# Weights of a slot by plain transfers with a register's row number, and w2 split one slot ahead

## The chip, the cores and the metric

The kernel runs on one core of a Trainium2 chip. The metric is the device time of one execution in microseconds (us). The matrix unit (TensorE) is called PE here, VectorE DVE, ScalarE ACT, GpSimd POOL and SyncE SP.

## The reference

Four attention problems are computed whose softmax runs over channels, and the result goes through a mixture of experts. Tokens with a positive skip score are computed, each by the one expert that its gate prefers; the others pass unchanged.

```python
s = kn.transpose(0, 2, 1) @ qn / tau          # q, k normalised over tokens; 256 x 256 per problem
a = softmax(s); x = (v @ a).reshape(20224, 256)
do_compute = x @ w_skip > 0
e_idx, gate_w = argmax and largest softmax of x[do_compute] @ w_gate     # 8 experts
for e in range(8):
    h = np.maximum(xc[mask] @ w1[e], 0.0)     # w1[e] 256 x 1024
    y[mask] = gate_w[mask] * (h @ w2[e])      # w2[e] 1024 x 256
out[do_compute] = xc + y
```

## The kernel before, in words

The program has three parts.

**The planned part.** All work up to the first loop is written as tasks with costs, dependences and due times (class `Plan`), and a planner puts them in an order per engine before the program is built. It covers the attention (scores, softmax, products with v), the routing of each token to its expert, lists of tokens per expert in DRAM (`lst`), and 7 blocks of 512 tokens of the expert with the most tokens so far. At its end DVE computes tables of slots (`tables`): a slot is a run of tokens of one expert. `adi` holds where a slot's list begins, `wii` which rows of the weight arrays belong to it.

**The large loop** (line 432, `Large.loop`) runs over slots of 1024 tokens, in two halves of 512. It ran 6 times in the profile shown. `first` is x times w1 with ReLU, `second` is h times w2. Float32 operands are split into a high and a low part (`w1H`, `w1L`, `w2s`), by a cast on ACT and a subtraction on DVE, so that each product needs three matmuls.

**The small loop** (line 522, `Small.loop`) runs over the rest, in slots of up to 128 tokens, two slots (u = 0, 1) in an iteration. It ran 5 times, so 10 slots. A slot has two stages. In the first, 32 matmuls multiply by w1 (`v1r`, line 539, result `ph`), and ACT and DVE make `yH` and `yL` of the result. In the second, 16 matmuls multiply by the split w2 (`v2s`, lines 558 and 559, result `po`), with the next slot's rows transposed in their midst (line 494), and DVE adds the result to the rows (`yo`, lines 564 and 565).

**Where weights come from.** Each slot's w1 and w2 are 128 x 2048 float32, 1 MB each. They are fetched by `gather_w`, an indirect transfer that POOL issues: each partition gives its own row number (`wc`, `wd`), which DVE has copied out of `wii`. Where a slot has the same expert as the slot whose buffer it takes over, `wii` holds a number out of bounds, and nothing is moved. Token rows come by `gather_x` (`yg`, line 209) and go back by `scatter_x` (`out`, line 214), on POOL too. SP only loads the lists (`load_list`, line 227), whose place it reads into a register.

**What sets the order in the loops.** The bodies are written out in order, per engine, and cut into four stages by `tc.stage_boundary()`: in the small loop, each slot's two. No engine enters a stage before all engines have ended the stage before the last one, and a stage has ended on the engine that issues transfers only when they have landed. `behind(...)` says at which point of a stage an engine reports that the stage before has ended. Ahead of each loop, and behind it, all engines wait for each other.

In the small loop before, w2 of a slot is split (`split_w2`) in that slot's own first stage, into a single `v2s`. w2 of the next slot is gathered at the start of the first stage, w1 of the slot after next at the start of the second.

Of the kernel before, what the change touches and what calls it, by code (L numbers as in the profile page):

```python
# [20 lines left out]
P = 128  # L21
# [122 lines left out]
def attn_moe(ctx: ExitStack, tc: tile.TileContext, q, k, vt, tau, w_skip, w_gate, w1, w2, out):  # L144
# [83 lines left out]


# [9 lines left out]
    class Large:  # L239
# [126 lines left out]
        def ahead(self, cnt0):  # L366


            V.scalar_tensor_tensor(cnt0, cnt0, 512.0 * K0, iota8, ALU.is_ge, ALU.mult)
            e0 = tab.tile([P, 1], F32, name="e0")  # L370
            V.tensor_reduce(e0, cnt0, AX.X, ALU.min)
            start = tab.tile([P, E], F32, name="start")
            V.tensor_scalar(start, iota8, e0, 512.0 * K0, ALU.is_equal, ALU.mult)
            V.tensor_scalar(e0, e0, float(E), None, ALU.add)
            ad0 = tab.tile([P, 1], I32, name="ad0")
            V.tensor_scalar(ad0, e0, float(CAP), None, ALU.mult)
            V.tensor_scalar(e0, e0, float(E - 1), None, ALU.min)
            for w in (self.wc, self.wd):
                V.tensor_scalar(w, e0, float(P), pidx, ALU.mult, ALU.add)
            yield e0, start  # L380
            beside(load_list(ad0, 0, self.lN[:, : 4 * K0, :], 4 * K0, G), "first lists", "later lists")
            yield
# [33 lines left out]
        def next_loads(self, adi, wii):  # L416

            self.adi, self.wii = adi, wii
            for w in (self.wc, self.wd):
                V.tensor_copy(w, wii[:, 0:1])  # L420
            yield
            load_list(adi, 0, self.lN[:, :8, :], 8)
            yield
            self.take(0)
            gather_w(w1, self.w1r, self.wc)
            self.gather(0)
            yield
            gather_w(w2, self.w2r, self.wd)
            yield

        def loop(self):
            with tc.For_i(0, self.n, 1, iteration_sync="staggered", hint_engines=(mybir.EngineType.PE,)) as i, tc.manual_schedule():
                V.tensor_copy(self.wc, self.wii[:, ds(i + 1, 1)])
                V.tensor_copy(self.wd, self.wii[:, ds(i + 1, 1)])
# [3 lines left out]
                gather_w(w1, self.w1r, self.wc)  # L438
# [4 lines left out]
                gather_w(w2, self.w2r, self.wd)  # L443
# [21 lines left out]
    class Small:  # L465


        def __init__(self, adi, wii):
            self.adi, self.wii = adi, wii
# [4 lines left out]
            self.xg = tiles([P, C], F32, "yg")  # L474
            self.xr = tiles([P, C], F32, "yr")
            self.xT = tiles([P, 2, P], F32, "yT")
            self.w2s = wp.tile([P, NFB, 2, C], F32R, name="v2s")
            self.hH = wp.tile([P, NFB, P], F32R, name="yH")
            self.hL = wp.tile([P, NFB, P], F32R, name="yL")
            self.ob = tiles([P, C], F32, "yo")  # L480
            self.wc = tiles([P, 1], I32, "vc")
            self.wd = tiles([P, 1], I32, "vd")
# [4 lines left out]
            for u in range(U):  # L487
                V.memset(self.xg[u], 0.0)
                V.memset(self.ob[u], 0.0)
# [8 lines left out]
        def split_w2(self, u, c):  # L498
            f = slice(c * 2, c * 2 + 2)
            r = self.w2r[u][:, c * 512 : (c + 1) * 512].rearrange("p (f c) -> p f c", c=C)  # L500
            S.copy(self.w2s[:, f, 0, :], r)
            V.tensor_tensor(self.w2s[:, f, 1, :], r, self.w2s[:, f, 0, :], ALU.subtract)

        def load_rows(self):
# [5 lines left out]
            for u in range(U):  # L510
                V.tensor_copy(self.wc[u], self.wii[:, u : u + 1])
                V.tensor_copy(self.wd[u], self.wii[:, u : u + 1])
                gather_x(self.xg[u], first[u][:, 0, :])

        def load_weights(self):
            for u in range(U):
                gather_w(w1, self.w1r[u], self.wc[u])
                if u < U - 1:
                    gather_w(w2, self.w2r[u], self.wd[u])

        def loop(self):
            with tc.For_i(0, self.n, U, iteration_sync="staggered") as i, tc.manual_schedule():  # L522
                for u in range(U):
# [3 lines left out]
                    gather_w(w2, self.w2r[o], self.wd[o])  # L527
# [3 lines left out]
                    for g in range(2):  # L531
                        for c in (0, 1, 2) if g == 0 else (3,):
                            self.split_w2(u, c)
# [10 lines left out]
                        if g == 0:  # L544
                            behind(T, S, V, SP)
                            V.tensor_copy(self.wc[u], self.wii[:, ds(i + (u + U), 1)])
                            V.tensor_copy(self.wd[u], self.wii[:, ds(i + (u + U), 1)])
# [5 lines left out]
                    gather_w(w1, self.w1r[u], self.wc[u])  # L553
                    gather_x(self.xg[u], self.lN[u][:, 0, :])
                    behind(G)
                    po = psum["o", u % 2].tile([P, 512], F32, name="po")
                    for f in range(NFB):
                        T.matmul(po, self.hH[:, f, :], self.w2s[:, f, :, :], start=(f == 0), stop=False, skip_group_check=True)
                        T.matmul(po[:, :C], self.hL[:, f, :], self.w2s[:, f, 0, :], start=False, stop=(f == NFB - 1), skip_group_check=True)
# [267 lines left out]
    def tables(e0, start):  # L827
# [20 lines left out]
        for i, (ns, w, back) in enumerate(((S8, 1024, 1), (S1, 128, U))):  # L848
# [6 lines left out]
            if i == 1:  # L855
                V.tensor_scalar(ei[:, :U], ei[:, :U], float(E - 1), None, ALU.min)
# [21 lines left out]
            V.tensor_tensor(same[:, back:], ei[:, back:], ei[:, : ns - back], ALU.is_equal)  # L878
            if i == 0:
                V.tensor_tensor(same[:, 0:1], ei[:, 0:1], e0, ALU.is_equal)  # L880
            else:
                V.memset(same[:, :back], 0.0)
# [133 lines left out]
    large = Large()  # L1016
    rows, early, slots, nexts, smalls = large.ahead(cnt0), [], [], [], []
# [68 lines left out]
    def table_part():  # L1086
        if not slots:
            early.append(tables(*early[0]))
# [3 lines left out]
    for n, cost in enumerate((1.64, 0.7, 1.5, 1.2, 1.49, 1.9, 1.6)):  # L1092
# [6 lines left out]
    def next_part():  # L1099
        if not nexts:  # L1100
            nexts.append(large.next_loads(slots[0][0], slots[1][0]))
        next(nexts[0])

    n0 = add("V", 0.15, next_part, [t1, wg2])
    n1 = add("D", 0.1, next_part, [n0, listed, in_order["gat"]])
    n2 = add("G", 5.4, next_part, [n1, stored[NC - 1], *w1s, puts.get(K0 - 3)])
    n2d = add("D", 4.4, None, [n2])
    n3 = add("G", 1.05, next_part, [n2, done[K0 - 1]], due=now)
# [3 lines left out]
    split_weights(1, n2d, last_m1, due=now)  # L1112

    def open_small():
        in_b.close()
        smalls.append(Small(slots[0][1], slots[1][1]))
        smalls[0].load_rows()
# [6 lines left out]
    add("G", 3.2, lambda: smalls[0].load_weights(), [sm, n3], due=now + 5)  # L1124
# [8 lines left out]
    with tc.manual_schedule():  # L1133
# [9 lines left out]
        smalls[0].transposed(0)  # L1143
        smalls[0].n = slots[3]
        large.loop()
        keep_warm(6)
        smalls[0].loop()
# [37 lines left out]
```

## Time and profile before

| | us |
|---|---|
| median of 3 runs (lowest to highest) | 840.38 (836.22 to 846.71) |
| the profiled execution | 839.25 |
| its span, first to last instruction | 837.6 |
| PE busy in the span | 792.3 (95%) |
| large loop, six slots, first matmul at | 469.46 |
| small loop, ten slots, first matmul at | 752.65 |

The span is about 1.7 us shorter than the execution's own time. PE is busy nearly throughout, so a gain has to come from the places where it isn't: the ends of the three parts, and the small loop.

### The profile page before, as it was taken

Reading aid. Unit: us, or ns where it says so; the run is one execution under the profiler, and the core shown is the slowest. Engines: PE = TensorE matmul, PEld = TensorE weight load, DVE = VectorE, ACT = ScalarE, POOL = GpSimd, SP = SyncE. Lnnn points to the kernel's source line nnn. Section 1 sums busy time; section 2 is a strip of 40 time slices with the busy share of each in tenths; the row PEclk is TensorE's granted clock in tenths of the full one; section 3 lists DMA queues with packets and bytes.
Section 4 is the critical chain, followed back from the end, with each engine's and each line's share of the span. In section 5 each row is a group of like instructions: output and inputs, shape, how many; then the busy total and the mean of one; then the engine's idle time right before and its main releaser. Section 6 shows DMA issues by size and latency. Waiting matters only on the chain. (4 is left out here: it accounts for less than half of the span.)

```text
span 837.6 us, 13567 instructions
## 1 busy us (share of the span) xinstructions
PE 792.3 (95%) x4506; PEld 697.6 (83%) x4506; DVE 519.4 (62%) x1055; ACT 369.5 (44%) x583; POOL 431.4 (52%) x470
## 2 busy tenths in 40 slices
PE   7999999989989999999989799999999999988886
PEld 5888998979978888998878588888888888877876
DVE  4729759968958653654556646556555647456555
ACT  5449558749746323433313324233333324234544
POOL 3000377767577757556764653435343443426666
PEclk9999999999999999999999899999999999999999
DMA  8969869979554342420601511111111111107670
GB/s 321 394 247 365 330 211 316 402 272 361 179 176 127 104 126 65 138 89 27 173 8 46 191 54 47 44 44 51 50 44 44 51 50 34 41 26 256 251 274 4
DMA packets 58074, 126.37 MB, mean 151 GB/s; under 512 B 17556, under 2 KB 37804, under 8 KB 55472
## 3 DMA queue, kind: packets, MB, share of 16 engines
q1 hardware_dynamic: 17280, 62.99, 20.3%
q0 software_dynamic: 19520, 42.12, 15.2%
q10 hardware_dynamic: 21232, 20.72, 8.1%
q8 instruction: 23, 0.38, 0.2%
q14 instruction: 19, 0.16, 0.1%
HBM read 115.98 MB, written 32.59 MB: 177 GB/s over the span
## 5 line engine op out<-in xcount | busy, mean ns | idle before, releaser
L817 POOL DMA_INDIRECT lst<-pay,r_posi x160 | 181.4, 1134 | 171.4 <-DVE r_posi L814 123.8
L662 PE MATMUL s<-qt,kt 128*128 128x256 f32 x640 | 148.3, 384 | 6.9 <-DMA kt<-in_k 6.9
L214 POOL DMA_INDIRECT out<-xg,lc x78 | 79.3, 1016 | 130.2 <-DVE xg L345 113.1
L662 PEld LDWEIGHTS s<-qt,kt 128*128 128x128 f32 x640 | 119.7, 192 | 22.3 <-issue 7.2
L338 PE MATMUL po<-w2s,hH 128*128 128x512 f32 x384 | 136.5, 399 | 0.4 <-issue 0.4
L321 ACT ACTIVATE hH<-ph 128x512 fp32r<-128x512 f32 x96 | 57.5, 599 | 129.6 <-PE ph L318 129.6
L339 PE MATMUL po<-w2s,hL 128*128 128x256 f32 x384 | 107.2, 279 | 0.0
L735 PE MATMUL px<-aH,vH 128*128 128x266 f32 x320 | 99.8, 312 | 0.6 <-ACT xo L742 0.6
L322 DVE SCALAR_TENSOR_TENSOR hL<-ph,hH 128x512 fp32r<-128x512 f32 x96 | 66.4, 692 | 54.7 <-ACT hH L321 53.3
L209 POOL DMA_INDIRECT xg<-out,lc x80 | 84.0, 1049 | 30.4 <-issue 18.7
L737 PE MATMUL px<-aH,vL 128*128 128x266 f32 x320 | 93.1, 291 | 0.0
L736 PE MATMUL px<-aL,vH 128*128 128x266 f32 x320 | 92.7, 290 | 0.3 <-DVE aL L719 0.3
L338 PEld LDWEIGHTS po<-w2s,hH 128*128 128x128 f32 x384 | 72.1, 188 | 17.4 <-issue 0.8
L338 PE MATMUL px<-w2s,hH 128*128 128x512 f32 x224 | 79.9, 398 | 2.4 <-DVE hL L401 2.4
L316 PE MATMUL ph<-xH,w1H 128*128 128x512 f32 x192 | 76.0, 396 | 5.0 <-issue 5.0
L742 ACT COPY xo<-px 128x532 f32<-128x532 f32 x80 | 47.7, 602 | 66.1 <-PE px L737 66.0
L317 PE MATMUL ph<-xL,w1H 128*128 128x512 f32 x192 | 75.6, 394 | 0.0
L318 PE MATMUL ph<-xH,w1L 128*128 128x512 f32 x192 | 75.5, 393 | 0.0
L339 PEld LDWEIGHTS po<-w2s,hL 128*128 128x128 f32 x384 | 72.4, 188 | 0.4
L284 ACT CAST xH<-pt 128x512 fp32r<-128x512 f32 x40 | 22.3, 590 | 106.1 <-PE pt L282 106.0
L735 PEld LDWEIGHTS px<-aH,vH 128*128 128x128 f32 x320 | 62.0, 194 | 2.0 <-ACT xo L742 1.0
L339 PE MATMUL px<-w2s,hL 128*128 128x256 f32 x224 | 63.6, 284 | 0.0
(206 smaller groups left out, 1588.3 us busy)
## 6 DMA issues: line engine op xcount, KB each, us to landing
vf<-in_vt SPq DMA_DIRECT2D x32, 640.0 KB, 6.6
qt<-in_q SPq DMA_DIRECT2D x31, 640.0 KB, 7.5
kt<-in_k SPq DMA_DIRECT2D x31, 640.0 KB, 7.4
out<-xo ACTq DMA_DIRECT2D x12, 1280.0 KB, 7.0
lst<-pay,r_posi POOLq DMA_INDIRECT x160, 4.2
out<-xo ACTq DMA_DIRECT2D x4, 640.0 KB, 5.3
out<-xo ACTq DMA_DIRECT2D x4, 576.0 KB, 8.0
xg<-out,lc POOLq DMA_INDIRECT x80, 2.8
```

Source lines behind the costliest of these rows:

```text
L209: apart(G.indirect_dma_start(out=to, out_offset=None, in_=out[0:n, :], in_offset=IndirectOffsetOnAxis(ap=ls[:, 0:1], axis=0), bounds_check ...
L214: i = (G.indirect_dma_start(out=out, out_offset=IndirectOffsetOnAxis(ap=ls[:, 0:1], axis=0), in_=src, in_offset=None, bounds_check=NTOK - ...
L316: T.matmul(ph, self.w1H[:, fs], self.xH[:, kb, :], start=(kb == 0), stop=False)
L317: T.matmul(ph, self.w1H[:, fs], self.xL[:, kb, :], start=False, stop=False)
L318: T.matmul(ph, self.w1L[:, fs], self.xH[:, kb, :], start=False, stop=(kb == 1))
L338: T.matmul(po, self.hH[:, f, ts], self.w2s[:, f, :, :], start=(f == 0), stop=False, skip_group_check=True)
L339: T.matmul(po[:, :C], self.hL[:, f, ts], self.w2s[:, f, 0, :], start=False, stop=(f == NFB - 1), skip_group_check=True)
L662: T.matmul(sums[b][:, cb, :], kt[:, j % JH, cb * P : (cb + 1) * P], qt[:, j % JH, :], start=(ch == 0 and j == 0 and cb == 0), stop=(ch == ...
L735: T.matmul(px[:, i, :NA], vH[:, kb, js], aH[:, kb, :], start=(kb == 0), stop=False)
L736: T.matmul(px[:, i, :NA], vH[:, kb, js], aL[:, kb, :], start=False, stop=False)
L737: T.matmul(px[:, i, :NA], vL[:, kb, js], aH[:, kb, :], start=False, stop=(kb == 1))
L817: i = G.indirect_dma_start(out=lst, out_offset=IndirectOffsetOnAxis(ap=posi[:, t : t + 1], axis=0), in_=pay[:, t0 + t, :], in_offset=None, ...
```

## The change

Weights of slots are no longer gathered by POOL. `load_w` reads the slot's first row number into a register of SP and issues a plain transfer of 128 rows. `wii` now holds expert x 128, never out of bounds: each slot's weights are fetched, whatever the slot before had. Beyond the last slot the last expert's are fetched. The row numbers on DVE (`wc`, `wd`) and the comparison of experts are gone.

In the small loop `v2s` has two buffers. A slot's w2 is split in the second stage of the slot before, among the `po` matmuls, and slot 0's ahead of the loop. Transfers of w2 and of w1 both go to the slot after next. The transposes of the next slot stand one matmul pair earlier. The zeroing of row buffers moves to the program's start.

```diff
+    def load_w(ei, i, src, to):
+        a = nc.sync.value_load(ei[0:1, ds(i, 1)], min_val=0, max_val=(E - 1) * P)
+        nc.sync.dma_start(to, src[ds(a, P), :])
...
@@ Large.loop
-                V.tensor_copy(self.wc, self.wii[:, ds(i + 1, 1)])
-                V.tensor_copy(self.wd, self.wii[:, ds(i + 1, 1)])
                 self.put_last()
                 self.take(1)
                 self.gather(1)
-                gather_w(w1, self.w1r, self.wc)
+                load_w(self.ei, i + 1, w1, self.w1r)
                 behind(G, SP)
                 self.first(True)
                 tc.stage_boundary()
                 load_list(self.adi, i + 1, self.lN[:, :8, :], 8)
-                gather_w(w2, self.w2r, self.wd)
+                load_w(self.ei, i + 1, w2, self.w2r)
...
@@ Small.loop
+            for c in range(4):
+                self.split_w2(0, c)
             with tc.For_i(0, self.n, U, iteration_sync="staggered") as i, tc.manual_schedule():
...
-                    gather_w(w2, self.w2r[o], self.wd[o])
+                    load_w(self.ei, i + (u + U), w2, self.w2r[u])
                     G.tensor_copy(self.ls[o], self.lc[o])
                     scatter_x(self.ls[o][:, 0, :], self.ob[o])
                     behind(G)
                     for g in range(2):
-                        for c in (0, 1, 2) if g == 0 else (3,):
-                            self.split_w2(u, c)
...
                     tc.stage_boundary()
                     G.tensor_copy(self.lc[o], self.lN[o])
                     G.tensor_copy(self.lN[o], self.lP[o])
+                    load_w(self.ei, i + (u + U), w1, self.w1r[u])
                     load_list(self.adi, i + (u + 2 * U + 1), self.lP[o], 1)
                     behind(SP)
-                    gather_w(w1, self.w1r[u], self.wc[u])
                     gather_x(self.xg[u], self.lN[u][:, 0, :])
                     behind(G)
                     po = psum["o", u % 2].tile([P, 512], F32, name="po")
+                    for c in range(2):
+                        self.split_w2(o, c)
+                    behind(S, V)
                     for f in range(NFB):
...
+                        if f == 3:
+                            self.transposed(o)
+                            for c in range(2, 4):
+                                self.split_w2(o, c)
                         if f == 4:
-                            self.transposed(o)
-                            behind(T, S, V)
+                            behind(T)
...
@@ tables
-            wi = tab.tile([P, ns], F32, name=f"wi{i}")
-            V.tensor_scalar(wi, ei, float(P), pidx, ALU.mult, ALU.add)
-            same = tab.tile([P, ns], F32, name=f"same{i}")
...
-            V.scalar_tensor_tensor(wi, same, float(BIG), wi, ALU.mult, ALU.add)
             wii = tab.tile([P, ns], I32, name=f"wii{i}")
-            V.tensor_copy(wii, wi)
+            V.tensor_scalar(wii, ei, float(E - 1), float(P), ALU.min, ALU.mult)
...
@@ the planned part's end
+    nw = add("D", 2.9, lambda: load_w(slots[1][0], 0, w1, large.w1r), [t1, *w1s])
+    add("D", 2.9, lambda: load_w(slots[1][0], 0, w2, large.w2r), [nw, *w2s])
...
-    add("G", 3.2, lambda: smalls[0].load_weights(), [sm, n3], due=now + 5)
+    for u in range(U):
+        for w in (1, 2):
+            add("D", 2.9, lambda u=u, w=w: small.load_weights(u, w), [sm], due=now + 5)
```

How instructions move is seen on the engines' own orders. First SP in the first slot of the small loop, before (what an instruction waits for stands in brackets; `sem_stage` is the stage count, `DMAHW` and `DMASW` are the semaphores of transfers from SP or ACT and from POOL):

```order
L226 ISA [waits DMAHW7_49,SP_sequencer_49,sem_stage_3_6615]
L226 TENSOR_LOAD adi_4800
L226 ISA x2
L227 ISA
L227 DMA mP_4840<-lst 128x2 [waits Pool_I-5467_stg1,DMAHW5_49]
```

And with the change (`v2r` is the raw w2, `v1r` w1, `mP` the list):

```order
L231 TENSOR_LOAD wii_4821 [waits SP_sequencer_49]
L231 ISA x2
L232 ISA
L232 DMA v2r_4830<-in_w 128x2048 [waits DMAHW2_49,DVE_49,Activation_49]
L231 ISA [waits SP_sequencer_49,DMAHW5_49,DMAHW6_49,sem_stage_3_6681]
L231 TENSOR_LOAD wii_4821
L231 ISA x2
L232 ISA
L232 DMA v1r_4828<-in_w 128x2048 [waits PE_I-5510_stg0,DMAHW1_49]
L226 TENSOR_LOAD adi_4819
L227 DMA mP_4843<-lst 128x2 [waits Pool_I-5510_stg1,DMAHW7_49]
L231 ISA [waits DMAHW0_I-5510_stg0,SP_sequencer_I-5510_stg0,sem_stage_0_6678]
```

Three transfers stand there instead of one. The w2 transfer waits for the split on DVE, w1 for the slot's `ph` matmuls, and SP reports a stage as ended only when they have landed (the two rows with `sem_stage`).

Second, DVE in a slot of the small loop, before (the subtractions of line 502 are w2's split):

```order
L502 TENSOR_TENSOR v2s<-v2r_4821,v2s 128x2x256 [waits sem_stage_0_6612,Activation_I-5467_stg2]
L502 TENSOR_TENSOR v2s<-v2r_4821,v2s 128x2x256 [waits Activation_I-5467_stg2] x2
L543 SCALAR_TENSOR_TENSOR yL<-ph,yH 128x512 [waits Activation_I-5467_stg2]
L546 COPY vc_4834<-wii_4811 128x1 [waits DMASW3_49]
L547 COPY vd_4836<-wii_4811 128x1
L502 TENSOR_TENSOR v2s<-v2r_4821,v2s 128x2x256 [waits Activation_I-5467_stg2]
L543 SCALAR_TENSOR_TENSOR yL<-ph,yH 128x512 [waits Activation_I-5467_stg2]
L564 SCALAR_TENSOR_TENSOR yo_4832<-po,mc_4842,yr_4825 128x256 [waits sem_stage_1_6613,DVE_I-5467_stg2,PE_49]
L565 SCALAR_TENSOR_TENSOR yo_4832<-po,mc_4842,yo_4832 128x256 [waits DVE_49]
```

And with the change:

```order
L534 SCALAR_TENSOR_TENSOR yL<-ph,yH 128x512 [waits sem_stage_0_6678,Activation_I-5510_stg2]
L534 SCALAR_TENSOR_TENSOR yL<-ph,yH 128x512 [waits DVE_I-5510_stg1,Activation_I-5510_stg2]
L498 TENSOR_TENSOR v2s_4836<-v2r_4830,v2s_4836 128x2x256 [waits sem_stage_1_6679,Activation_49]
L498 TENSOR_TENSOR v2s_4836<-v2r_4830,v2s_4836 128x2x256 [waits Activation_49]
L498 TENSOR_TENSOR v2s_4836<-v2r_4830,v2s_4836 128x2x256 [waits DVE_I-5510_stg2,Activation_49]
L498 TENSOR_TENSOR v2s_4836<-v2r_4830,v2s_4836 128x2x256 [waits Activation_49]
L559 SCALAR_TENSOR_TENSOR yo_160<-po,mc_4845,yr_4833 128x256 [waits PE_49]
L560 SCALAR_TENSOR_TENSOR yo_160<-po,mc_4845,yo_160 128x256 [waits DVE_49]
```

The four subtractions moved behind both `yL`, and ahead of `yo`: a slot's result now stands behind the next slot's split.

Third, SP at the end of the planned part, behind the five list loads that it had before, with the change:

```order
L227 DMA mP_4842<-lst 128x2
L231 TENSOR_LOAD wii_4821
L231 ISA x2
L232 ISA
L232 DMA v1r_4828<-in_w 128x2048
L231 TENSOR_LOAD wii_4821
L232 DMA v2r_4830<-in_w 128x2048
L231 TENSOR_LOAD wii_4821
L232 DMA v1r_4829<-in_w 128x2048
L231 TENSOR_LOAD wii_4821
L232 DMA v2r_4831<-in_w 128x2048
L430 COMPARE_AND_BRANCH
```

Four loads of weights stand between SP's last list and the point where all engines meet ahead of the large loop (the branch).

## Rows read from the trace of the kernel before

**Rows 1.** Windows: large loop, gated small slots, plain loads; times, busy, clock, DMA, GB/s.
```profile
511.00:735.00 224.00, 224.00 (x1171) 191.44 (x1170) 128.10 (x223) 75.89 (x134) 92.75 (x100) 1.00 0.15 45
767.50:809.50 42.00, 34.47 (x250) 31.65 (x251) 23.89 (x50) 20.11 (x41) 25.41 (x36) 1.00 0.69 258
17.00:44.00 27.00, 27.00 (x127) 23.77 (x126) 19.40 (x18) 13.31 (x11) 0.00 (x0) 1.00 1.00 396
```

**Rows 2.** Timeline, PE, small loop: start, length, instruction, idle before with releaser.
```profile
752.65 3.81 PE L539 MATMUL ph<-yT,v1r 128*128 128x128 f32 x32 [1.45 <-DVEq L522]
...
767.53 3.81 PE L539 MATMUL ph<-yT,v1r 128*128 128x128 f32 x32
772.83 0.47 PE L558 MATMUL po<-v2s,yH 128*128 128x512 f32 x1 [1.49 <-DVE v2s L502]
...
817.53 3.81 PE L539 MATMUL ph<-yT,v1r 128*128 128x128 f32 x32
821.09 0.48 PE L558 MATMUL po<-v2s,yH 128*128 128x512 f32 x1
...
824.59 3.73 PE L539 MATMUL ph<-yT,v1r 128*128 128x128 f32 x32
```

**Rows 3.** Waits of PE in the small loop: total us, times, longest.
```profile
PE po L558 <- DVE v2s L502: 5.9, 5, 1.7
PE po L558 <- DVE yL L543: 2.9, 2, 1.5
```

**Rows 4.** Timeline, DVE: the last split of w2 in the slots of rows 2.
```profile
771.63 0.68 DVE L502 TENSOR_TENSOR v2s<-v2r,v2s 128x512 fp32r<-128x512 f32 x1
...
821.67 0.68 DVE L502 TENSOR_TENSOR v2s<-v2r,v2s 128x512 fp32r<-128x512 f32 x1
```

**Rows 5.** Timeline, POOL, from one slot's second stage to the next's.
```profile
773.22 0.19 POOL L549 COPY mc<-mN 128x2 int32<-128x2 int32 x1
...
774.43 1.05 POOL L221 DMA_INDIRECT v1r<-in_w,vc  x1 [0.70 <-issue]
...
780.98 0.18 POOL L549 COPY mc<-mN 128x2 int32<-128x2 int32 x1 [0.67 <-DMA yg<-out,mN]
```

**Rows 6.** Transfers: issues, KB each, median us to landing; v1r's under its tile.
```profile
vf<-in_vt SPq DMA_DIRECT2D x2, 640.0 KB, 3.9
...
out<-yo,ms POOLq DMA_INDIRECT x10, 3.7
...
DMA to landing us min/median/max: 5.5/7.6/9.6
```

**Rows 7.** Lines, small loop: busy us, mean ns of one, idle before.
```profile
L502 DVE TENSOR_TENSOR v2s<-v2r,v2s 128x512 fp32r<-128x512 f32 x40 | 25.8, 685 | 5.9 <-ACT v2s L501 5.9
L501 ACT CAST v2s<-v2r 128x512 fp32r<-128x512 f32 x40 | 22.7, 615 | 11.2 <-SPq L522 8.8 <-PE po L559 1.8 <-issue 0.5
```

**Rows 8.** Timeline between the two loops: PE's warming matmuls, ACT's first split.
```profile
749.62 1.58 PE L1131 MATMUL m<-ones 128*128 128x128 f32 x12 [1.25 <-PEq L432]
...
752.34 1.66 ACT L501 CAST v2s<-v2r 128x512 fp32r<-128x512 f32 x3 [8.85 <-SPq L522]
```

**Rows 9.** Timeline, the end: the last result on DVE, its scatter on POOL.
```profile
831.95 0.48 DVE L565 SCALAR_TENSOR_TENSOR yo<-po,mc,yo 128x256 f32<-128x256 f32 x1
...
833.46 1.00 POOL L214 DMA_INDIRECT out<-yo,mc  x1 [1.07 <-PEq L1181]
```

**Rows 10.** Timeline ahead of the large loop, and the window of its first matmuls.
```profile
459.83 1.49 SPq L227 DMA_DIRECT2D mN<-lst  x2
462.08 1.45 SPq L227 DMA_DIRECT2D mP<-lst  x2
...
466.38 0.48 DVE L345 SCALAR_TENSOR_TENSOR xg<-px,lc,xg 128x256 f32<-128x256 f32 x1
...
469.46 0.77 PE L316 MATMUL ph<-xH,w1H 128*128 128x512 f32 x1 [5.03 <-issue]
...
469.40:474.00 4.60, 4.54 (x11) 3.60 (x12) 0.92 (x2) 1.10 (x2) 3.69 (x4) 0.50 0.93 340
```

More of the change, by code (lines that the diff above doesn't have):

```diff
@@ L379, in ahead @@
                 V.tensor_scalar(w, e0, float(P), pidx, ALU.mult, ALU.add)
-            yield e0, start
+            yield start
             beside(load_list(ad0, 0, self.lN[:, : 4 * K0, :], 4 * K0, G), "first lists", "later lists")
@@ L465, in attn_moe, with __init__, open @@
     class Small:
-        def __init__(self, adi, wii):
-            self.adi, self.wii = adi, wii
+        def __init__(self):
+            tiles = lambda name: [const.tile([P, C], F32, name=f"{name}{u}") for u in range(U)]
+            self.xg, self.ob = tiles("yg"), tiles("yo")
+            for x in (*self.xg, *self.ob):
+                V.memset(x, 0.0)
+        def open(self, adi, ei):
+            self.adi, self.ei = adi, ei
             wp = ctx.enter_context(tc.tile_pool(name="ws", bufs=1, side="right", reuse_waits="tile"))
@@ L486, in __init__ @@
             self.ls = tiles([P, 1, 2], I32, "ms")
-            for u in range(U):
-                V.memset(self.xg[u], 0.0)
-                V.memset(self.ob[u], 0.0)
         def transposed(self, u):
@@ L825, in route, with tables @@
                 yield
-    def tables(e0, start):
+    def tables(start):
         cnt = tab.tile([P, E], F32, name="cnt")
@@ L847, in tables @@
         yield
-        for i, (ns, w, back) in enumerate(((S8, 1024, 1), (S1, 128, U))):
+        for i, (ns, w) in enumerate(((S8, 1024), (S1, 128))):
             ns += 2 * U + 2
@@ L1015, in attn_moe @@
     cnt0 = tab.tile([P, E], F32, name="cnt0")
-    large = Large()
-    rows, early, slots, nexts, smalls = large.ahead(cnt0), [], [], [], []
+    large, small = Large(), Small()
+    rows, early, slots = large.ahead(cnt0), [], []
     look = add("V", 1.6, lambda: early.append(next(rows)), [based[D0 - 1]])
@@ L1087, in table_part @@
         if not slots:
-            early.append(tables(*early[0]))
+            early.append(tables(early[0]))
         next(early[-1])
     t = based[NC - 1]
-    for n, cost in enumerate((1.64, 0.7, 1.5, 1.2, 1.49, 1.9, 1.6)):
+    for n, cost in enumerate((1.64, 0.7, 1.5, 0.25, 1.49, 1.9, 0.3)):
         t = add("V", cost, table_part, [t, *(in_order["hL", 3] if n == 4 else [])])
@@ L1097, in attn_moe, with next_list @@
             t1 = t
[L1099 to L1108, printed above, removed]
+    def next_list():
+        large.adi, large.ei = slots[0][0], slots[1][0]
+        large.next_list()
+    n1 = add("D", 0.1, next_list, [t1, wg2, listed, in_order["gat"]], wait=2.0)
+    n2 = add("G", 5.6, large.next_rows, [n1, stored[NC - 1], puts.get(K0 - 3)])
+    n2d = add("D", 0.4, None, [n2], wait=1.5)
+    nw = add("D", 2.9, lambda: load_w(slots[1][0], 0, w1, large.w1r), [t1, *w1s])
+    add("D", 2.9, lambda: load_w(slots[1][0], 0, w2, large.w2r), [nw, *w2s])
     tr = rows_ready(K0, n2d)
@@ L1111, in attn_moe @@
         x.due = min(x.due, now - 3)
-    split_weights(1, n2d, last_m1, due=now)
+    split_weights(1, nw, last_m1, due=now)
     def open_small():
         in_b.close()
-        smalls.append(Small(slots[0][1], slots[1][1]))
-        smalls[0].load_rows()
+        small.open(slots[0][1], slots[1][1])
+        small.load_rows()
     def counts():
@@ L1142, in attn_moe @@
         psum["o", 1] = ctx.enter_context(tc.tile_pool(name="ps_o1", bufs=1, space=PSUM, side="right"))
-        smalls[0].transposed(0)
-        smalls[0].n = slots[3]
+        small.transposed(0)
+        small.n = slots[3]
         large.loop()
         keep_warm(6)
-        smalls[0].loop()
+        small.loop()
 def kernel(q, k, v, tau, moe_w_skip, moe_w_gate, moe_w1, moe_w2):
```

47 lines of the change are left out of this document (11 added, 36 removed).

## The prediction

> **What bounds the kernel now.** I read the windows first, to see in which part PE is idle, then PE's timeline there, then what ended its waits. In the large loop PE is busy 224.00 of 224 us at full clock, and the DMA engines only 0.15 [rows 1]: neither POOL's gathers there nor their removal can move it. In the small loop it is different: in 42 us of it PE is busy 34.47 [rows 1]. So the change is worth what the small loop's idle time is worth, plus what it does to the two places where all engines meet.
>
> A small slot without a wait takes 7.06 us (817.53 to 824.59), and `po` begins 3.56 us after `ph`. In a slot with a wait `po` begins 5.30 us after (767.53 to 772.83), with 1.49 us idle [rows 2]. Those waits add up to 5.9 + 2.9 = 8.8 us in 7 of the 10 slots [rows 3]. The profile names DVE's split of w2 and `yL` as their ends, and the reader should doubt it: in the slot with the wait the last split ended 772.31, 4.78 us after `ph` began; in the slot without, 822.35, 4.82 us after [rows 4]. DVE was equally late in both, and PE started `po` without it in one. What differs is the transfers. POOL's first copy of a second stage stands at 773.22, the w1 gather is issued at 774.43, and the next second stage opens at 780.98, 6.55 us after that issue [rows 5]; landing takes 5.5 to 9.6 us [rows 6]. As a stage opens only when the transfers of the stage before the last have landed, the loop turns at the speed of this chain: 1.2 us to the gather, 6.5 us to its landing. The late slots without a wait are the last ones, for which weights beyond the end are asked for, out of bounds.
>
> **The change, part by part.**
>
> *Small loop, w1.* SP needs about 1.13 us to read a register and issue: two such loads lie between 459.83 and 462.08 [rows 10]. Then 1 MB. A plain 640 KB load landed in 3.9 us [rows 6], at the 396 GB/s that plain loads sustained [rows 1] 1.66 us of it moving data, so 2.2 us fixed; 1.05 million bytes are then 2.65 + 2.2 = 4.9 us. Chain: 1.13 + 4.9 + about 0.3 for the report = 6.3 us, under the 7.06 that PE needs. This gate goes.
>
> *Small loop, w2.* It gets a wait: for DVE's split, which now ends after the casts. ACT's second ReLU ends about 4.45 us into a slot; two casts, the two row copies and two casts more bring it to about 7.4, and DVE's last subtraction (0.685 us [rows 7]) to 8.25. The transfer lands at 8.25 + 0.15 + L and has to be in before the next-but-one slot opens, 0.3 us for the report: the pitch P is at least (8.7 + L) / 2. With L = 4.9 that is 6.8, with two times 0.33 us more for the 128 KB of the row gather and of the scatter at the same 396 GB/s, 7.15. Queued behind it on SP are only w1 and the list, which wait for the same stage anyway.
>
> *Small loop, results.* `yo` stands behind two more subtractions, its scatter with it. It has the same formula with 9.2 us for the end of `yo`: 2P = 9.2 + 0.3 + 3.7 + 0.3, P = 6.75, with the landing of 3.7 us [rows 6]. All three chains lie between 6.3 and 7.15, PE itself at 7.06. **I take P = 7.1**; bounds 6.8 (the last slot's own work, 824.59 to the first `yo` of about 831.4) and 8.15 (L as long as today's 7.6).
>
> Here a rule speaks against the change. The page DMA: Bandwidth & Descriptors of the Trainium skill, section Issuing engines are not separate DMA queues, says that transfers of all issuing engines run on the same 16 engines, and that another issuer saves issuing time alone. By it the chain of about 8.2 us (rows 5, with the start of the stage) would shorten by the gather's 1.05 us only, to some 7.1, and the slots that waited for nothing would take that too; the rows of plain loads give 6.8. The saving would be 6.7 us by the first and 9.4 by the second.
>
> *Small loop, sum.* Now from 752.65 to the end of the last `yo`, 832.43 [rows 2, 9]: 79.78 us. After: nine pitches of 7.1, and the last slot, 7.84 now (824.59 to 832.43), plus two subtractions of 0.685 ahead of `yo`, 9.21. Together 73.1: **6.7 us less.**
>
> *Ahead of the small loop.* Slot 0's split stood inside the slot, hidden beside `ph`; now four casts and four subtractions stand between the loops. The engines are let out of the large loop at about 749.6 [rows 8]; the first cast takes 0.6, then 4 x 0.685, so DVE is done at about 753.0. Today the last to come is PE with its warming matmuls, done at 751.20, and `ph` follows 1.45 us later. Bounds 0 (if DVE counts when its last instruction is issued and barely later) and 1.8; I take **+1.2**.
>
> *Ahead of the large loop.* SP was through with its lists at 463.53, DVE's last result came at 466.86, PE began at 469.46 [rows 10]. Four weight loads at 1.13 put SP at 468.05: it becomes the last. POOL loses four gathers of about 1.3 us and DVE the zeroing, neither of which is then waited for. Bounds -0.5 and +1.3 (SP's coming takes 2.6 us as DVE's does); I take **+0.3**.
>
> *Costing nothing.* The large loop's 12 transfers more, 1 MB each, two in a slot of some 45 us: the engines there are 0.15 busy [rows 1], and the buffers were free a stage before. If that cover were gone it would show as PE idle there. DVE's fewer copies; POOL's fewer gathers. Beyond the last slot two more pairs of weights are fetched: they land before the last scatter (833.46) has.
>
> *Total:* -6.7 + 1.2 + 0.3 = -5.2 us. The profiled execution took 839.25; 834.1 after. It lay 1.1 under the median, so **835** for the median.
>
> **The rivals.**
>
> *Slower: w2's landing becomes the gate.* The place is the SP row that waits for w2 before a slot may open. For: each slot now fetches both weights, where equal experts had let some go; 2.36 MB in 7.1 us is 332 GB/s against 258 today, and in the queue of SP w2 stands behind w1. Against: plain loads sustained 396 [rows 1]. It decides from P = 7.67, where 9P + 9.21 + 1.5 reaches 79.78, so from L = 6.65 us. At L = 7.6, today's median [rows 6], P = 8.15 and the loop with its entries takes 84.1: 4.3 us more, 844.7.
>
> *The scatter gate.* If the scatter of `yo` lands 1.5 us later than today, as it shares the engines with w2, P = 7.5: the total is -1.6 us, 838.8. The page DMA: Bandwidth & Descriptors, section Queues, rings and completion order, has each engine go round the queues packet by packet, by which small rows move in among the weights; today they stand in one queue.
>
> *The clock falls between the loops.* PE idles 1.45 us there now and 2.65 then. After 5.03 us of idling ahead of the large loop its granted clock was 0.50 for 4.6 us [rows 10], the lower level; that costs half of it, 2.3 us: 837.5. The page TensorE: Matmul & The Clock Gate, section on the HAM clock gate, has an idle array fall back to 1.2 GHz; the row agrees.
>
> *More gain.* If POOL's lighter load lets the large loop start early enough that the clock does not fall there, 2.3 us and the earlier start of 1 us are won on top: 831.9. Against: SP is late instead.
>
> *The change doesn't do what it says* would be gathers left on POOL or a split left before `po`; the orders show neither, so it has no chance of its own.
>
> **How the numbers follow.** Forecast 0.58; slower by w2's landing 0.17; scatter gate 0.10; clock 0.10; more gain 0.05. Runs of before lay between 4.2 under and 6.3 over their median, so each case is blurred by some 3 us. The range 829.5 to 842.5 takes in the forecast with P from 6.8 to 7.4, the clock, the scatter gate and the lower half of the slower case. 2% of 840 is 17 us, about what a measurement here can tell from no change, and more than the whole idle time of the small loop: faster 0.02, same 0.96, slower 0.02.
>
> **What would show it.** Right: PE's waits ahead of `po` gone, slots at about 7.1 us, `ph` of the first slot about 1.5 us later against the large loop's end, the large loop unchanged. Wrong: PE waiting ahead of `ph` or `po` with SP's weights landing at that moment (P near 8), or matmuls of the first slot at half clock. The forecast fails if L is over 6.6 us, or if the waits were DVE's after all: then they would go with the split, and P would still fall, but with w1 landing late and nobody waiting.

## The result, and the profile after

The changed kernel's median is 831.48 us (829.91 to 840.5), that of before on the same chip 841.95 us (836.22 to 846.71), 20 runs each; the ratio is 0.9886, 95% interval 0.9865 to 0.9907. That is 10.5 us less where 5.4 were forecast, inside the range, and under 2%. The two profiled executions differ by less: 839.25 and 833.26 us, spans of 837.6 and 831.6.

Where the 6.0 us between the spans came from is told by cutting both traces at the same work: the end of PE's part ahead of the loops, the first and the last matmul of the large loop, the first `ph` of the small loop, the end of its last `yo`. All in us:

| | before | after | difference | forecast |
|---|---|---|---|---|
| planned part, to PE's last matmul | 464.44 | 463.02 | -1.4 | 0 |
| PE idle ahead of the large loop | 5.02 | 5.35 | +0.3 | +0.3 |
| large loop, PE from first to last | 278.91 | 278.43 | -0.5 | 0 |
| between the loops | 4.28 | 5.39 | +1.1 | +1.2 |
| small loop, first `ph` to last `yo` | 79.78 | 74.87 | -4.9 | -6.7 |
| behind the last `yo` | 5.17 | 4.54 | -0.6 | 0 |

The small loop first. Windows of it, before and then after (times, sum of PE, PEld, DVE, ACT and POOL, granted clock, DMA share, GB/s), beside the 42 us of [rows 1]:

```profile
752.60:832.40 79.80, 69.18 (x500) 62.95 (x500) 48.07 (x100) 39.72 (x80) 51.54 (x71) 1.00 0.57 207
```

```profile
752.20:827.10 74.90, 68.91 (x500) 64.09 (x500) 47.63 (x80) 39.03 (x80) 26.15 (x50) 0.98 0.81 291
```

POOL's busy time is halved, the transfers have risen from 207 to 291 GB/s, and the clock's mean is no longer 1.00. PE's timeline after (start, length, instruction, idle before it and what ended it), which answers to [rows 2]:

```profile
748.15 1.58 PE L1116 MATMUL m<-ones 128*128 128x128 f32 x12 [1.34 <-PEq L430]
...
752.19 5.44 PE L530 MATMUL ph<-yT,v1r 128*128 128x128 f32 x32 [2.46 <-DVE v2s L498]
...
760.48 3.73 PE L530 MATMUL ph<-yT,v1r 128*128 128x128 f32 x32
...
768.28 3.81 PE L530 MATMUL ph<-yT,v1r 128*128 128x128 f32 x32 [1.03 <-DVE v2s L498]
...
796.95 3.81 PE L530 MATMUL ph<-yT,v1r 128*128 128x128 f32 x32 [1.20 <-DVE v2s L498]
...
803.68 3.73 PE L530 MATMUL ph<-yT,v1r 128*128 128x128 f32 x32
...
811.54 3.81 PE L530 MATMUL ph<-yT,v1r 128*128 128x128 f32 x32 [1.13 <-DVE v2s L498]
```

And PE's waits in the small loop, in answer to [rows 3] (total us, times, longest):

```profile
PE ph L530 <- DVE v2s L498: 5.8, 4, 2.5
PE ph L530 <- ACT v2s L497: 0.5, 1, 0.5
```

Three things are to be seen. No row speaks of `po`: the waits of 8.8 us are gone. A new wait of 0.5 to 1.2 us stands ahead of `ph` in every second slot: slots take 6.7 and 7.3 to 8.0 us in turn, 7.22 on the mean without the first. And the first `ph` took 5.44 us, where it took 3.81 before: PE had idled 2.46 us ahead of it, and this is the clock there, beside that of the large loop's start, which is the same as in [rows 10]:

```profile
468.40:473.00 4.60, 4.60 (x11) 3.68 (x12) 1.01 (x2) 1.10 (x2) 1.95 (x2) 0.51 1.00 411
752.10:757.50 5.40, 5.31 (x33) 5.34 (x34) 0.69 (x1) 0.60 (x1) 1.57 (x5) 0.68 0.57 222
```

A mean of 0.68 is part of the stretch at the lower of the two levels. The difference of 5.44 - 3.81 = 1.63 us is nearly all of the 1.8 us that the small loop lacks to its forecast of 73.1.

Ahead of the large loop, SP's loads and PE's first matmul (timeline), which answer to [rows 10]; DVE's last result there ended at 464.62:

```profile
463.03 0.33 SPq L232 DMA_DIRECT2D v1r<-in_w  x1
464.14 0.33 SPq L232 DMA_DIRECT2D v2r<-in_w  x1
465.35 0.33 SPq L232 DMA_DIRECT2D v1r<-in_w  x1
466.46 0.33 SPq L232 DMA_DIRECT2D v2r<-in_w  x1
...
468.37 0.77 PE L321 MATMUL ph<-xH,w1H 128*128 128x512 f32 x1 [5.35 <-PEq L430]
```

From DVE's end PE now needs 3.75 us, where it needed 2.60 [rows 10]: DVE is no longer what it waits for, SP's last load comes 1.8 us after it. From the end of that load's issue, 466.79, to PE's first matmul it is 1.58 us. In the ten traces with plain loads, on all chips, this distance is 1.49 to 1.62 us, while that from DVE's last result is 3.74 to 6.16 us: it is SP that sets the start. Of the 1.15 us that PE loses there, 0.8 are won back, as DVE's last result comes 1.60 us behind PE's part ahead of the loops, where it came 2.42 behind it before.

### The profile page after: what moved, and what is told of

The parts are those of the page before. It is cut to its first block, busy times and chain, and to the rows that moved or that the text cites. A ratio compares the mean times of both kernels' runs of the same rounds, so it can differ in the third digit from the quotient of the medians.

```text
span 831.6 us, 13722 instructions
## 1 busy us (share of the span) xinstructions
PE 790.9 (95%) x4506; PEld 697.8 (84%) x4506; DVE 518.3 (62%) x1012; ACT 370.4 (45%) x587; POOL 388.3 (47%) x433
```

## The experiments

They were run in three groups on three chips. On those of the first and the third group the kernel before took a median of 927 and 919 us, with a mean granted clock of about 0.95 over the whole execution (0.99 on the first chip), and on that of the second 836.94. The total times of one kernel spread over 9 to 32 us on these chips. In the traces the part ahead of the loops ends at 461 to 469 us on the second chip and at 537 to 553 on the two others, while the large loop takes 278.2 to 279.6 on all of them, so each reading below is a stage of the trace, cut as in the table above; "from the planned part on" is the span less that part: 373.16 us before, 368.58 after.

**1. The kernel before with no weights to land** (`b1_all_skipped`):

```
 if i == 0: V.tensor_tensor(same[:, back:], ei[:, back:], ei[:, : ns - back], ALU.is_equal)
+else:      V.memset(same[:, back:], 1.0)
```

> The kernel before, with every weight gather of the small slots from the third on sent out of bounds, so that it moves nothing (its instructions stay; the small slots then compute with the first weights). Landing theory (the waits ahead of `po` are stages that open late because a weight gather has not landed): the 8.8 us of waits ahead of `po` go to under 1 us, slots take about 7.06 us, the small loop 9 x 7.06 + 7.8 = 71.4 us in place of 79.78, and the time falls by about 8 us. Split theory (PE waits for DVE's split of w2 and for yL, as the profile names them): neither has become earlier, the waits stay at about 8.8 us and the time within 1 us.

Neither. The loop moved 25 GB/s in place of 207 and took 76.22 us: slots of 7.5 us, not 7.06 and not 8.1, with 5.9 us of waits ahead of `po` (2.0 of them in one slot near the end). POOL's timeline shows what is left, here a slot of 7.92 us from copy to copy (slots are 7.1 and 7.9 us in turn on POOL, 7.5 on the mean):

```profile
875.40 0.69 POOL L549 COPY mc<-mN 128x2 int32<-128x2 int32 x1
876.23 0.18 POOL L550 COPY mN<-mP 128x2 int32<-128x2 int32 x1
877.11 1.04 POOL L221 DMA_INDIRECT v1r<-in_w,vc  x1 [0.70 <-DVE yL L543]
878.46 1.01 POOL L209 DMA_INDIRECT yg<-out,mN  x1 [0.31 <-issue]
879.78 1.33 POOL L221 DMA_INDIRECT v2r<-in_w,vd  x1 [0.30 <-issue]
881.11 0.37 POOL L528 COPY ms<-mc 128x2 int32<-128x2 int32 x1
882.30 1.02 POOL L214 DMA_INDIRECT out<-yo,ms  x1 [0.82 <-POOL ms L528]
883.32 0.20 POOL L549 COPY mc<-mN 128x2 int32<-128x2 int32 x1
```

POOL never waits for as much as 1 us here: its four transfers and three copies fill the slot, with gathers that move nothing as dear to issue as real ones. So before, two gates lay close together: POOL's own row of instructions at 7.5 us, and, with real transfers, their landing at 8.08. The landing was 0.5 us a slot of the loss, not all of it. The 7.5 us are a reading of this trace, in which the token rows still land; no run took instructions off POOL and left the gathers' landing. Before, in the slot of [rows 2] with the wait, the landing is seen on POOL:

```profile
772.12 1.09 POOL L214 DMA_INDIRECT out<-yo,ms  x1 [2.29 <-DMA yg<-out,mN]
```

POOL waits for the token rows `yg`, which stand behind w1 in its queue, until 772.12, and `po` follows 0.71 us later. POOL waited so in three of the seven slots in which PE waited ahead of `po`, with `po` 0.71 to 0.75 us behind; in the others POOL waits less than 1 us.

**2. The kernel before with no gather skipped** (`b2_none_skipped`; `memset(..., 0.0)` in the line above):

> The kernel before, with no weight gather of the small slots left out for an equal expert (the whole 1 MB is fetched for each slot that has an expert). Landing theory: waits ahead of `po` in every slot but the last ones, pitch about 8.2 us, small loop about 9 x 8.2 + 7.8 = 81.6 us, so 1 to 4 us slower. Split theory: no change, within 1 us.

The small loop took 80.74 us at 205 GB/s, 16.6 MB, against 79.78 us and the same 16.6 MB before. Nothing was tried by this: in these data the skip for an equal expert never came into play in the small loop, only the numbers beyond the last slot did.

**3. Plain loads alone** (`b3_plain_only`, and again as `c2_plain_again`):

```
 load_w(..., i + (u + U), w2, self.w2r[u])  ->  load_w(..., i + (u + 1), w2, self.w2r[o])
 self.w2s = tiles(...)                      ->  self.w2s = wp.tile(...)   # one buffer
-for c in range(4): self.split_w2(0, c)     # ahead of the loop
 the four split_w2(u, c) back ahead of ph in their own slot
```

> The changed kernel with its second part undone: weights by plain transfers of SyncE, but w2 split in its own slot into one buffer, ahead of `po`, as before. Landing theory: the plain load of w1 lands early enough (1.13 + 4.9 + 0.3 = 6.3 us, under 7.06), so the waits ahead of `po` go although the split stands where it stood; slots 7.06 us, small loop about 71.5 us, no splits between the loops, so 7 to 8 us under before and 1 to 3 us under the changed kernel. Split theory: the waits ahead of `po` stay (about 8.8 us), the time within 2 us of before; the gain comes from splitting ahead.

> The kernel with plain loads alone (w2 split in its own slot, one buffer), on the same chip as the changed kernel. On another chip its small loop took 73.02 us and nothing stood between the loops. If the second part of the change costs more than it brings: the small loop again 72.5 to 73.5 us, the first `ph` at 3.8 us, the entry to it 1.1 us shorter than in the changed kernel, together about 3 us under the changed kernel. If splitting ahead is what the plain loads need: waits ahead of `po` of 5 us or more and a time equal to or over the changed kernel's.

Two more things stand as before in this kernel: the place of the transposes and of `behind`, and three loads of weights, not four, ahead of the large loop. The waits fell as the landing theory had it, but not to nothing: small loops of 73.02 and 72.47 us (71.5 expected), slots of 7.25 and 7.17, first `ph` 3.81 us, 4.32 and 4.33 us between the loops, and waits ahead of `po` of 3.2 and 2.9 us in all, where there were 8.8. From the planned part on it took 367.78 and 367.56 us; the changed kernel on the chip of the second took 370.75 (below). DVE's last split of a slot in the first of the two traces, and PE in the same slot:

```profile
854.90 0.68 DVE L498 TENSOR_TENSOR v2s<-v2r,v2s 128x512 fp32r<-128x512 f32 x1
```

```profile
850.79 3.73 PE L530 MATMUL ph<-yT,v1r 128*128 128x128 f32 x32
854.64 0.47 PE L547 MATMUL po<-v2s,yH 128*128 128x512 f32 x1
```

The split ends 4.79 us after `ph` begins, as late as in the slot of before with a wait of 1.49 us (4.78, [rows 2, 4]), and here `po` follows 3.85 us after `ph`, before that split is done, and no wait is shown ahead of it: the first matmul of `po` reads the first quarter of `v2s`, the last split makes the fourth. The split that the profile named was not the cause.

**4. Splitting ahead alone** (`b4_ahead_only`): the gathers stay on POOL, `wd[o]` is filled a slot earlier, the split stands as in the change.

> The kernel before with the second part of the change alone: GpSimd's gathers stay, w2 is split a slot ahead into two buffers (and its gather moves two slots ahead). Landing theory: the w1 gather still lands after 5.5 to 9.6 us, so waits of about the same size stay (ahead of `po`, or ahead of `ph`, wherever the stage opens late), and slot 0's split between the loops adds 1.2 us: 0 to 4 us slower than before. Split theory: the waits go, small loop about 72 us, 6 to 7 us faster.

The waits stayed, 10.4 us ahead of `po`, under other names (the last column is the idle time and what ended it):

```profile
865.09 0.47 PE L562 MATMUL po<-v2s,yH 128*128 128x512 f32 x1 [1.56 <-ACT yH L543]
868.20 3.73 PE L540 MATMUL ph<-yT,v1r 128*128 128x128 f32 x32
873.18 0.47 PE L562 MATMUL po<-v2s,yH 128*128 128x512 f32 x1 [1.25 <-ACT yH L543]
```

Small loop 82.35 us, mean slot 8.16, and 5.30 us between the loops, 1.0 more than before. So the second part of the change alone brings nothing: it costs 1.0 us between the loops, and the small loop is 2.6 us longer than before, 1.7 of it in the last slot (9.58 for 7.84), and 1.6 longer than in experiment 2 on the same chip. The rest of this kernel's time cannot be compared: a copy into `wd[0]` that I added ahead of the loops had to wait for a gather to land, and DVE stood for 9.21 us:

```profile
556.98 0.15 DVE L520 COPY vd<-wii 128x1 int32<-128x1 int32 x1 [9.21 <-DMA v2r<-in_w,vd]
```

**5. What the new wait ahead of `ph` hangs on.** Three edits of the changed kernel.

```
a1: the second pair of split_w2(o, c) behind the two yo instructions
a2: G.tensor_copy(self.ls[o], self.lc[o])  ->  G.memset(self.ls[o], BIG)
a3: load_w(..., w2, self.w2r[u])           ->  load_w(..., w2[:, : C], self.w2r[u][:, : C])
```

> The changed kernel with the second pair of w2 splits behind `yo` in place of ahead of it: `yo` and its scatter come about 1.4 us earlier, the last split (and with it the issue of the next w2 load) about as much later. What the waits of 0.5 to 1.2 us ahead of `ph` in every second slot hang on: if on the landing of the scatter of `yo`, they go and the loop is 3 to 5 us shorter (pitch 6.9 to 7.0); if on the landing of w2, they grow by 0.7 to 1.4 us in every second slot, 4 to 6 us slower; if on neither (the turn of the loop itself), no change but for the last slot's `yo`, 1.4 us earlier.

> The changed kernel with the scatters inside the small loop sent out of bounds (results of nine small slots are not written). If the waits ahead of `ph` hang on the scatter's landing, they go: 3 to 5 us faster. If on w2's landing: the scatter shares the engines, so 0 to 1.5 us. If on the turn of the loop: no change.

> The changed kernel with a quarter... an eighth of each w2 (its first 256 of 2048 columns, 128 KB in place of 1 MB) loaded inside the small loop. If the waits ahead of `ph` hang on w2's landing, they go: 3 to 5 us faster, slots about 6.75 us. If on the scatter: it lands sooner with the engines free, 0 to 3 us. If on the turn of the loop: no change.

PE's waits in the small loop of a1, then of a3:

```profile
PE ph L530 <- DVE yo L558: 3.3, 3, 1.1
PE ph L530 <- DVE v2s L498: 2.5, 1, 2.5
PE po L550 <- issue: 1.0, 3, 0.5
PE ph L530 <- DVE yo L557: 0.9, 1, 0.9
```

```profile
PE ph L530 <- DVE v2s L498: 2.5, 1, 2.5
PE po L550 <- issue: 1.5, 4, 0.5
```

With w2 an eighth as long all waits ahead of `ph` inside the loop go; only the entry's 2.5 is left. The mean slot is 6.89 us and the small loop 72.25, of which the first `ph` took 5.44 at the lower clock again. With `yo` ahead of the split, so with w2's load later and the scatter earlier, slots grew to 7.52 and the loop to 76.30, 1.4 more where w2's theory had 4 to 6. Without scattered rows the loop took 71.51 us with a first `ph` of 3.81, 1.4 to 1.6 under the two runs below that had this too.

By these totals w2's landing looks like the gate. The landings themselves say something else. Here are the w2 load and the scatter ahead of the wait of 1.20 us that ended at 796.95 in the changed kernel, and how long each took to land:

```profile
790.47 0.33 SPq L232 DMA_DIRECT2D v2r<-in_w  x1
DMA to landing us min/median/max: 4.8/4.8/4.8
791.52 1.00 POOL L214 DMA_INDIRECT out<-yo,ms  x1 [2.55 <-DVE yo L560]
DMA to landing us min/median/max: 4.7/4.7/4.7
```

And the same in a1, scatter first, with the `ph` that had waited 0.86 us:

```profile
796.07 1.19 POOL L214 DMA_INDIRECT out<-yo,ms  x1 [1.37 <-DVE yo L558]
DMA to landing us min/median/max: 2.5/2.5/2.5
797.13 0.33 SPq L232 DMA_DIRECT2D v2r<-in_w  x1
DMA to landing us min/median/max: 4.8/4.8/4.8
802.58 3.81 PE L530 MATMUL ph<-yT,v1r 128*128 128x128 f32 x32 [0.86 <-DVE yo L557]
```

In the changed kernel the scatter landed last, at 796.17, and w2 at 795.24; in a1 the scatter at 798.62 and w2 at 801.90. Sixteen waits ahead of `ph` (the changed kernel, c1, a2 and a4, four each) end 0.71 to 0.78 us behind the scatter's landing, whereas w2's, where the trace has it, lies 0.9 to 1.7 us ahead of them. The four of a1 end 0.68 us behind w2's landing and 3.7 to 4.2 behind the scatter's. So in the changed kernel the gate was the scatter's landing, with w2's 0.2 to 0.9 us ahead of it, and a1 made w2's the later one. It took the scatter 3.9 to 4.7 us to land behind a load of 1 MB, 2.3 to 2.7 ahead of one (a1) and 2.1 to 2.4 beside one of 128 KB (a3). So a3 shortened both landings and could not tell them apart, and a2 removed neither: with all its rows out of bounds the scatter still landed after 3.9 to 4.2 us. The gain of a3, 2.6 us, is under the 3 to 5 expected, as PE's own 6.7 us is close below.

**6. The clock ahead of the first small slot** (`a4_warm`, `keep_warm(6)` to `keep_warm(10)`):

> The changed kernel with 10 warming matmuls between the loops in place of 6. They end about 1.05 us later, at the time at which DVE's splits of slot 0 end. If the first small slot's 5.44 us (others 3.7) is a clock that fell in PE's idle 2.46 us, granted clock 0.68 there, it comes back to 3.7 us with the idle at about 1.4 us, and the time falls by about 1.7 us. If the first slot is slow for another reason (weights of the first slot late), it stays.

PE's timeline:

```profile
755.40 2.47 PE L1116 MATMUL m<-ones 128*128 128x128 f32 x20 [1.34 <-PEq L430]
759.44 3.81 PE L530 MATMUL ph<-yT,v1r 128*128 128x128 f32 x32 [1.57 <-DVE v2s L498]
```

The warming takes 0.9 us longer, the idle time behind it is shorter by that, the first `ph` takes 3.81 us at a granted clock of 1.00, and the small loop 72.93 us: 1.94 less. The time between the loops is unchanged (5.38), as DVE was last there. From the planned part on, 367.50 us. The median of the whole time was 837.0, no less than before's 836.94 on that chip, on which the changed kernel itself has no run. The planned part of the profiled execution ended at 469.40; more on that below.

**7. The changed kernel once more, and the entry to the large loop** (`c1_changed_again`; `c3_one_read` is experiment 3, `c4_warm_one_read` experiment 6, each with one `value_load` for both weights of a slot ahead of the large loop):

> The changed kernel itself once more, on the chip on which the next ones run. The small loop, from the first `ph` to the end of the last `yo`, is again 74 to 75.5 us with new waits of about 1 us ahead of `ph` in every second slot, and the first `ph` takes 5.4 us if PE's clock falls in its idle 2.46 us (it did in three of the four profiles with such an idle time). The time is 5 to 10 us under before.

> The last kernel with one register read in place of two for slot 0's two weights ahead of the large loop. If SyncE, the last to arrive there, sets the start of the large loop, and a read takes most of the 1.11 us from one load's issue to the next, the large loop starts 0.5 to 0.8 us earlier against DVE's last result and the time falls by as much. If something else is last (DVE, the meeting itself), no change.

> The changed kernel with 10 warming matmuls in place of 6 and one register read for each small slot's two weights ahead of the large loop (two reads less). Small loop about 73 us (first `ph` 3.8 us), start of the large loop 1 to 1.5 us earlier against DVE's last result if SyncE sets it, together 2.5 to 3.5 us under the changed kernel; if it does not, 1.5 to 2 us under it.

The small loops came as expected: 74.42 us with a first `ph` of 5.44 behind an idle 2.46, then 72.95 and 73.13 with 3.81. The total of c1 did not: 917.81 us, a ratio to before of 0.9982 (0.9946 to 1.0019), so on this chip the gain in the whole time is not shown. For c2 and c3 it isn't either (0.9988 and 1.0009), for c4 it is (0.9921, 0.9882 to 0.9960). From the planned part on c1 took 370.75 us, against 374.6 in experiment 2, which moved what the kernel before moves, on a chip as slow. The entry is one reason. SP's loads of c1 ahead of the large loop, and PE's first matmul:

```profile
537.77 0.71 SPq L232 DMA_DIRECT2D v1r<-in_w  x1
541.38 0.00 SPq L232 DMA_DIRECT2D v2r<-in_w  x1
542.81 0.00 SPq L232 DMA_DIRECT2D v1r<-in_w  x1
543.28 0.33 SPq L232 DMA_DIRECT2D v2r<-in_w  x1
```

```profile
545.18 0.76 PE L321 MATMUL ph<-xH,w1H 128*128 128x512 f32 x1 [7.93 <-PEq L430]
```

Here the loads stand up to 3.6 us apart, not 1.1, and PE idles 7.93 us; with c2, c3 and c4, 7.25, 7.01 and 7.17, against 5.11 and 5.14 in experiments 1 and 2, kernels with gathers on a chip as slow. One read less brought 0.24 us (c2 to c3), two 0.76 (c1 to c4), and 0.52 and 0.75 against DVE's last result: the right sign, but one and the same kernel showed 6.98 and 7.25 on the two slower chips, so the size is not settled. That SP sets the start is: PE's first matmul came 1.49 to 1.57 us behind the end of SP's last issue in all four. From the planned part on: 370.75, 367.56 (c2), 367.19, 369.11 us.

## Why the prediction was right, and where it was not

*The total.* The forecast of -5.2 us against the profiled execution came out as -6.0, of which -1.4 lie in the planned part. PE's order of instructions is the same in both kernels there (DVE's and POOL's are not), and the 1.4 us are small beside what that part varies by (see the median, below), which leaves -4.6. Of these, the -0.6 behind the last `yo` is not shown to be the change's: that stage took 4.60 to 4.62 us with gathers too, in experiments 1, 2 and 4 on another chip.

*Waits ahead of `po` are landings, not DVE's split: right in what it denied, half right in what it named.* Experiments 3 and 4 refute the split from both sides. But by experiment 1 some 7.5 us would have been left without the weights' landing, from POOL's own instructions as its trace reads. I had reckoned POOL's gather as the start of the w1 chain only, and not added up its slot. It changed nothing in the sum, since plain loads take away both. And the landing of 5.5 to 9.6 us [rows 6], from which the slower rival had its 7.6, is that of two gathers issued at 465.24 and 467.84, ahead of the large loop: the trace has no landing of w1 in the small loop. The last packet of the gather issued at 774.43 ended 5.25 us after its issue.

*Pitch of 7.1: right,* 7.22, 7.16, 7.17 and 7.18 in the four traces of the change with whole transfers (a4's among them). But the chain that gave the number was not the one that held the loop, so part of this is luck. The 7.15 was w2's chain, with twice 0.33 us added for shared engines. Measured, w2 was issued 8.2 us into the slot before (8.4 forecast), landed in 4.7 to 4.9 and let PE go 0.68 us later (0.3 forecast, a term that no row stands behind): 6.8 us a slot, as the formula has it without that addition. The chain of the results, put at 6.75, was the longer one: the scatter came at 9.2 us (9.5 forecast), landed in 3.9 to 4.7 where today's 3.7 had been taken, and PE went 0.71 us later, so 6.9 to 7.3 us a slot in the traces of the changed kernel, c1, a2 and a4. That is the scatter gate of the rivals, for the reason given there (it shares the engines with w2), with 0.2 to 1.0 us in place of 1.5. The loads' landings of 4.8 to 5.0 us stood against an estimate of 4.9. The Trainium skill's page DMA: Bandwidth & Descriptors, section Issuing engines are not separate DMA queues, led to the same 7.1 by the issuing time of one gather. It calls what another issuer saves usually small, and that does not fit this loop: in experiment 1's reading POOL's issuing alone holds the slot at 7.5 us, where the plain loads end at 7.2 with all their bytes.

*Each slot "now fetches both weights, where equal experts had let some go": wrong.* Experiment 2 shows that none had been let go. The 5.25 MB by which the loop's transfers grew, from 16.56 to 21.81 MB, are five loads of 1.05 MB more, 20 for 15: six for slots beyond the end of the list, which the gathers had passed over as out of bounds, less w2 of slot 1, which now comes ahead of the loop.

*Between the loops +1.2: right,* +1.1. *Ahead of the large loop +0.3, SP last: right* on this chip and on the second (5.40 to 5.62 us), and from SP's coming to PE's start it was 1.5 to 1.6 us, not the 2.6 of the bound; on the two slower chips the entry took 6.98 to 7.93, against 5.11 and 5.14 with gathers, so +1.9 to +2.8, beyond the bound of 1.3.

*Large loop free: right,* 278.4 against 278.9 us.

*The clock between the loops: the step that failed.* I gave the fall 0.10 and 2.3 us, for an idle time of 2.65 us. It came in the changed kernel both times, and in a1 and a3, always behind 2.45 or 2.46 us; it did not behind 2.26 (a2), 1.57 or less, nor behind 2.47 in experiment 4, which is another kernel. So the length of the idle time alone does not tell, and 0.10 was too little. Its price was 1.63 us. The Trainium skill's page TensorE: Matmul & The Clock Gate, section on the HAM clock gate, has an idle array fall back to 1.2 GHz; those four traces agree, and the one of experiment 4 shows that an idle time of the same length need not bring it.

*The median.* 10.5 us between the medians is 4.5 more than between the profiles: before's profile lay 2.7 under its median, after's 1.8 over. In five executions of kernels with one and the same planned part (the changed kernel and a1 to a4) that part ended between 461.19 and 469.40 us, so the medians can differ by such an amount for reasons outside the change. The traces show where: at about 170 us ACT waits for a transfer of the attention's results, `out<-xo`, to land, DVE and PE behind it. Here are the shortest and the longest such wait (a3, then a4):

```profile
168.27 1.26 ACT L614 CAST vH<-vf 128x1280 fp32r<-128x1280 f32 x1 [1.16 <-DMA out<-xo]
173.96 1.26 ACT L614 CAST vH<-vf 128x1280 fp32r<-128x1280 f32 x1 [5.56 <-DMA out<-xo]
```

PE idles 0.21 us there in a3, 2.49 in the changed kernel, 2.54 before, and 3.08 to 4.61 in a1, a2 and a4; the granted clock from 170 to 185 us was 1.00 in the first two, 0.89 before and 0.77 to 0.89 in the last three. The -1.4 us of the planned part between the two profiles arose there as well, at idle times that are nearly equal. On the second chip the variants of the changed kernel seem to lie in two groups, some near 830 and more near 837 us. Why that transfer lands late in some executions, and whether the change has a part in it, stays open.

## What to carry to other kernels

A releaser's name in a profile is the last of several; the same instruction equally late in a slot without a wait clears it at no cost. When two transfers can hold a stage, look in each wait for the one that landed last, at a constant distance ahead: an edit that shortens both cannot tell. When an engine issues all transfers of a loop, add up its own instructions for one turn as well as the landing: skipped or empty gathers cost it the same time. And look at what a change puts between two stages: one microsecond there cost 1.6 more by the clock, and leaving that work out took back 3.2 us on the same chip (370.75 to 367.56, from the planned part on).

## What the runs showed of the hardware

- An indirect gather with all rows out of bounds still took POOL 1.04 us to issue (experiment 1), as long as one that moves 1 MB (1.05, [rows 5]). A scatter with all rows out of bounds still landed 3.9 to 4.2 us after its issue beside a load of 1 MB (a2).
- A scatter of token rows landed in 3.9 to 4.7 us when it was issued 1 us behind a plain load of 1 MB, and in 2.3 to 2.7 when it was issued 1 us ahead of one (a1).
- Plain loads of 1 MB issued by SP landed in 4.8 (w2) and 5.0 us (w1) on the median while the loop moved 291 GB/s on the mean.
- SP's register reads with loads, 1.1 us apart on one chip, stood 0.5 to 3.6 us apart on another with the same instructions. No run tells why.
